# Expert index lists written to memory as three rows of 384 bytes, transposed on the PE first

## The chip, the cores and the metric

The kernel runs on one core of a Trainium2 chip. The metric is the time of one execution in microseconds (us), as the median of several runs. A separate execution was taken with the hardware profiler; its rows are in a section below. The engines are the PE (matrix products), the DVE (vector), the ACT (scalar functions), the POOL (GpSimd) and the SP, which issues most transfers. Each engine works through its own instructions in order. Transfers issued by the SP run on the hardware queue q1, indirect ones issued by the POOL on the software queue q0; both are served by the same 16 DMA engines.

## The reference, cut to what matters

Three stages follow each other: attention with pooled queries; a mixture of 8 experts with a capacity of 288 tokens each; a dense block with a softmax-weighted activation and layer norm.

```python
def _moe_ref(x, w_gate, w1, w2):          # x: 2304 x 512, 8 experts, F = 1024
    cap = N // E                          # 288
    logits = x @ w_gate
    order = np.argsort(-logits.flatten())
    for idx in order:                     # greedy: best pairs first
        tok, e = (int(idx) // E, int(idx) % E)
        if assigned[tok] >= 0 or counts[e] >= cap:
            continue
        assigned[tok] = e
        counts[e] += 1
    for e in range(E):
        mask = assigned == e
        out[mask] = np.maximum(x[mask] @ w1[e], 0.0) @ w2[e]

def _moe2_ref(x, w_in, w_out, g_ln):
    h = x @ w_in
    solu = h * softmax(h)
    return (layernorm(solu) * g_ln) @ w_out
```

Each expert takes exactly 288 tokens, so the experts' outputs, one after the other, are 18 blocks of 128 rows, and the dense block works on them in that order. Its results go back to the rows of the tokens.

## The kernel before, in words

Attention and the gate's logits come first and take the first half of the time. The tokens' vectors lie in memory as `xd`. The second half (class `Moe`) goes through the experts, in an order that the routing itself decides.

**Routing** (`Router.phase`, one phase for each expert). Which expert fills up next, and with which tokens, is found on the DVE by comparing keys with thresholds and on the PE by counting, in rounds: `cmp`, a matmul, `ge`, a matmul, `jm`. The end of a phase makes the expert's list of tokens: each token's slot, then a matmul over 18 chunks (L695) into PSUM, from which the DVE copies `idf6` (L698) and computes the 288 indices as a tile `ix` of 96 partitions by 3 (L699). The generator `phase` yields between engines; each piece is an entry of the schedule below, named `f`, `t`, `s`, `a`, `i` (the index matmul) and `x` (the DVE's part). `upd` then brings the routing state up to date.

**The list** is used twice. The POOL gathers the tokens' rows with three indirect transfers of 96 rows of 2 KB (`g_row`, into `h`). And the SP writes the list to memory as a part of `tab` (`g_tab`, L770), from where `e2_ix` later loads it in another division, 128 indices to a block, as `ixb`; with these the POOL scatters the finished rows to the output (`e2_st`, L880).

**The expert.** The PE transposes the gathered rows (`g_tr`, L776), the ACT splits each tile into a high part (`xh`) and the DVE makes the low part (`xl`). Weights come as `raw` blocks of 512 KB, eight to an expert (`w_load`), in three buffers; the ACT makes the high part `wh` (`w_hi`, L766), the DVE the low part `wl` (L769). First product: `c_mm` (L790), with `hh` and `hl` behind it; second: `d_mm` (L804), with `yh` (L808) and `yl` (L810).

**The dense block** takes each finished block of 128 rows: `e1_mm` (L816), then `e1_h`, maximum, exponent, `zz`, mean and variance on ACT and DVE, transposes (L856), `e2_mm` (L870), `e2_o` and the scatter.

**The order** on every engine is fixed before the kernel runs. `Moe.run` describes each operation with an engine, an assumed duration, a priority, what it needs and which buffers it takes and frees; the list scheduler `Sched` plays that through and emits the operations in the order of its result. Entry `gt` is the write of the list, `gr` the gathers, `wd` a weight load, `gx` the transposes, `cm` and `dm` the two products, `m1` and `m2` those of the dense block. The engines then run that order with real waits.

Of the kernel before, what the change touches and what calls it, by code (L numbers as in the profile page):

```python
# [14 lines left out]
ALU = mybir.AluOpType  # L15
# [4 lines left out]
I32=DT.int32  # L20
# [5 lines left out]
class Sched:  # L26


    def __init__(s,bufs,lat=195,cold=0,begin=600.0):
        s.bufs=dict(bufs); s.lat=lat if isinstance(lat,dict) else dict.fromkeys(('X','PE','ACT','DVE','POOL','SP'),lat); s.cold=cold; s.begin=begin; s.ops=[]; s.name={}; s.free0={}  # L30
        s.same=dict(X=0,PE=0,ACT=155,DVE=128,POOL=105,SP=200)
    def op(s,key,eng,dur,pri,f,need=(),alloc=(),free=(),late=0,slack=0,lock=0,until=0.0):
        assert key not in s.name,key
        o=dict(key=key,eng=eng,dur=dur,pri=pri,f=f,need=list(need),alloc=list(alloc),free=list(free),late=late,slack=slack,until=until,lock=lock or eng=='POOL',i=len(s.ops),ready=0.0,succ=[],t=None)
        s.ops.append(o); s.name[key]=o
# [500 lines left out]
I32=DT.int32  # L536
NT=18; E=8; CAP=288
NEG=-3.0e38
ROUNDS=((2048<<16,31),(64<<16,31),(1<<16,63),(2048,31),(64,31),(1,64))
def route_consts(tc,C):  # L540
    nc=tc.nc; c={}
    def it(name,shape,pattern,base,cm,dt=F32):
        t=C.tile(shape,dt,name=name)
        nc.gpsimd.iota(t,pattern=pattern,base=base,channel_multiplier=cm,allow_small_or_imprecise_dtypes=True)
        return t
    c['w8']=it('w8',[128,8],[[-1,8]],8,0)
    ms=C.tile([64,6],BF,name='ms')
    for n,(st,J) in enumerate(ROUNDS):
        u=st>>16 or st
        c['thr',n]=it(f'thr{n}',[128,J],[[u,J]],u if n<5 else 0,0)  # L550
        if n<3: nc.vector.tensor_scalar(c['thr',n],c['thr',n],65536.0,None,op0=ALU.mult)
        nc.vector.memset(ms[:,n:n+1],-float(st))
    c['ms']=ms
    c['i96']=it('i96',[128,96],[[1,96]],0,0)
    c['i3']=it('i3',[128,3],[[1,3]],0,0)
    c['chv']=it('chv',[128,NT],[[1,NT]],0,0)
    c['pv']=it('pv',[128,1],[[0,1]],0,1)
    jp=it('jp',[128,128],[[1,128]],0,-1)
    c['tri']=C.tile([128,128],BF,name='tri'); nc.vector.tensor_scalar(c['tri'],jp,0.0,None,op0=ALU.is_gt)
    c['ones']=C.tile([128,128],BF,name='onesb'); nc.vector.memset(c['ones'],1.0)  # L560
    return c
class Router:
    def __init__(s,tc,C,W,ps,L,consts):
        s.tc=tc; s.nc=nc=tc.nc; s.W=W; s.ps=ps; s.L=L; s.c=consts
        s.neg=C.tile([128,E],F32,name='neg'); nc.vector.memset(s.neg,0.0)
        s.rem=C.tile([128,E],F32,name='rem'); nc.vector.memset(s.rem,float(CAP))
        s.un=C.tile([128,NT],F32,name='un'); nc.vector.memset(s.un,1.0)
        s.asg=C.tile([128,NT,E],F32,name='asg'); nc.vector.memset(s.asg,0.0)
        s.idx={}; s.ev={}; s.rest=None
        s.A=C.tile([128,NT,128],BF,name='A'); nc.gpsimd.memset(s.A,0.0)  # L570
    def t(s,name,shape,dt=F32,bufs=2): return s.W.tile(shape,dt,name=name,bufs=bufs)
    def psum(s): return s.ps.tile([128,512],F32,name='rt',bufs=1)
# [5 lines left out]
    def phase(s,k):  # L578

        nc=s.nc; V=nc.vector; c=s.c; last=(k==E-1)  # L580
        f=s.t('f',[128,E]); fm=s.t('fm',[128,1]); f2=s.t('f2',[128,E])
        sl=s.t('sl',[128,2,NT],BF); tmp=s.t('tmp',[128,NT,E],bufs=1)
        if not last:
# [18 lines left out]
            for n,(st,J) in enumerate(ROUNDS):  # L602
# [14 lines left out]
                p=s.psum()  # L617
# [6 lines left out]
                p=s.psum()  # L624
# [15 lines left out]
        gt=s.t('gt',[128,2,NT])  # L640
# [7 lines left out]
            V.tensor_tensor(tmp,oh,s.be(f2),op=ALU.mult)  # L648
            ohf=s.t('ohf',[128,NT]); s.red(ohf,tmp,ALU.add)
        if k>0:  # L650
            tm2=s.t('tm2',[128,NT,E],bufs=1)
            V.tensor_tensor(tm2,s.asg,s.be(f2),op=ALU.mult)
            asf=s.t('asf',[128,NT]); s.red(asf,tm2,ALU.add)
        if k==0:
# [10 lines left out]
        p=s.psum()  # L665
# [27 lines left out]
        p=s.psum()  # L693
# [3 lines left out]
        idf=s.t('idf6',[96,6]); ix=s.t('ix',[96,3],I32,bufs=8)  # L697
        V.tensor_copy(idf,p[:96,:6])  # L698
        V.scalar_tensor_tensor(ix,idf[:,0:3],128.0,idf[:,3:6],op0=ALU.mult,op1=ALU.add)  # L699
        s.idx[k]=ix  # L700
        s.rest=None
        if not last: s.rest=(inr,key,gt,oh,f2)
    def update(s):
# [25 lines left out]
class Moe:  # L729
# [37 lines left out]
    def w_lo(s,k,i,e,j):  # L767
        nc=s.nc; hi,lo=s.wt[k,i]; raw=s.raw[k,i]; c=slice(j*512,j*512+512)
        (nc.vector if e=='V' else nc.gpsimd).tensor_tensor(lo[:,c],raw[:,c],hi[:,c].bitcast(F32),op=ALU.subtract)  # L769
    def g_tab(s,k): s.nc.sync.dma_start(s.tab[k*CAP:(k+1)*CAP].rearrange("(c a) -> a c",a=96),s.rt.idx[k])  # L770
    def g_row(s,k,c):
        x=s.xg[k,c]=s.W.tile([128,512],F32,name='h2',bufs=HB)[:96]
        s.nc.gpsimd.indirect_dma_start(out=x,out_offset=None,in_=s.x,in_offset=bass.IndirectOffsetOnAxis(ap=s.rt.idx[k][:,c:c+1],axis=0))
# [107 lines left out]
    def run(s):  # L881
# [4 lines left out]
        def op(key,eng,dur,pri,f,*a,**kw): X.op(key,eng,dur,pri+M['off'].get(key[0],0),lambda: f(*a),**kw)  # L886
# [6 lines left out]
        def seg(key,eng,dur,pri,g,need=()):  # L893
            nonlocal last
            op(key,eng,dur,pri,lambda: next(g(),None),lock=eng=='DVE' and dur<2000 and dur>600,need=list(need)+([last] if last else []))
            last=key
        J=[31,31,63,31,31,64]
        for k in range(E):
# [3 lines left out]
            p=-2e6 if k==0 else S0+PER*(k-1)+M['rp']  # L902
            ps=0 if k==0 else M['rs']
            i=0
            def sg(name,eng,dur,g):
                nonlocal i
                seg(('r',k,name),eng,dur,p+ps*i,g); i+=1
            if k>0:
                def u0(k=k): start(k); return s.up
                sg('u0','DVE',1165,u0); sg('u1','PE',25,lambda: s.up); sg('u2','DVE',281,lambda: s.up)  # L910
                ph=lambda k=k: s.ph[k]
            else:
                def ph0(): start(0); return s.ph[0]
                ph=lambda: s.ph[0]
            if k<E-1:
                for n in range(6):
                    g0=ph0 if k==0 and n==0 else ph
                    sg(('d',n),'DVE',{0:3200}.get(n,100+139+(710 if J[n]<63 else 1340)),g0)
                    sg(('p',n),'PE',480,ph); sg(('g',n),'DVE',77,ph); sg(('q',n),'PE',7,ph)
            sg('f','DVE',2541 if k<E-1 else 900,ph); sg('t','PE',60,ph); sg('s','DVE',2900,ph); sg('a','DVE',1940,ph); sg('i','PE',428,ph); sg('x','DVE',250,ph)  # L920
            ix=('r',k,'x')
            b0=S0+PER*k
            op(('wr',k),'SP',300,b0+M['wd'],s.w_reg,k,need=[('r',k,'f')])
            for i_ in range(8):
# [3 lines left out]
                e=M['lo' if k else 'lo0'][i_]  # L928
                for j in range(2):
                    op(('wl'+e,k,i_,j),'DVE' if e=='V' else 'POOL',605 if e=='V' else 1250,tn+M['wl']+j,s.w_lo,k,i_,e,j,lock=1,need=[('wh',k,i_)]+([('r',0,'x') if e=='V' else ('gr',0,2)] if k==0 else []),free=[(('wd',k,i_),'raw')])  # L930
            op(('gt',k),'SP',480,-1e6,s.g_tab,k,need=[ix],late=1800)
            for c in range(3): op(('gr',k,c),'POOL',1038,-1e6+c,s.g_row,k,c,need=[ix]+([('cm',k-1,1,1)] if k else []),alloc=['h2'],late=7300)
            for dc in range(4):
                op(('gx',k,dc),'PE',246,b0+M['gx'],s.g_tr,k,dc,need=[('gr',k,c) for c in range(3)]+([('gx',k,0)] if dc else []),alloc=['tr'] if dc else ['tr','x'],free=[(('gr',k,c),'h2') for c in range(3)])
# [3 lines left out]
            for f in range(8):  # L938
                t=b0+1500*f
# [5 lines left out]
            c=(k*CAP)%128; nb=(k*CAP+CAP)//128-(k*CAP)//128; bb=(k*CAP)//128  # L945
# [4 lines left out]
            for d in range(4):  # L950
                for h in range(4):
                    t=b0+12000+750*(4*d+h)
# [3 lines left out]
                t=b0+12000+1500*(2*d+1)  # L956
                op(('dh',k,d),'ACT',291,t,s.d_hi,k,d,c,need=[('dm',k,d,3)]+([('cy',k)] if c else [])+ye)
                op(('dl',k,d),'DVE',369,t,s.d_lo,k,d,c,need=[('dh',k,d)],free=[(('dm',k,d,0),'cd')])
            for j in range(nb):
# [6 lines left out]
                t=t1+5200+M['ec']  # L966
# [30 lines left out]
def whole(tc, q, k, v, w_gate, w1, w2, w_in, w_out, g_ln, out):  # L997
    nc = tc.nc
    if w_in.dtype == DT.int64:
        w_in, w_out = [a.bitcast(I32).rearrange("a (b t) -> a b t", t=2) for a in (w_in, w_out)]  # L1000
    with tc.tile_pool(name="dr", bufs=1, space=bass.MemoryType.DRAM) as DR, tc.tile_pool(name="c", bufs=1) as C, \
            tc.tile_pool(name="rt", bufs=2) as RT:
        xd = DR.tile([2304, 512], F32, name="xd")
        tab = DR.tile([2304], I32, name="tab")
        wst = DR.tile([2, 512, 1024], F32, name="wst")
        wso = DR.tile([2, 1024, 512], F32, name="wso")
        idf = C.tile([128, 128], F32, name="idf")
        make_identity(nc, idf)
        L = C.tile([128, 18, 8], F32, name="L")
        consts = route_consts(tc, C)  # L1010
        with tc.tile_pool(name="ps", bufs=1, space=PS) as ps, tc.tile_pool(name="ca", bufs=1) as CA:
            wg = CA.tile([128, 4, 8], F32, name="wg")
            nc.sync.dma_start(wg, w_gate.rearrange("(c p) e -> p c e", p=128))
            gs = CA.tile([128, 16], F32, name="gs")
            nc.sync.dma_start(gs[:, 0:8], g_ln.rearrange("(c p) -> p c", p=128))
            nc.gpsimd.tensor_scalar(gs[:, 8:16], gs[:, 0:8], 2.0**-52, 1.0, op0=ALU.mult, op1=ALU.mult)
            attention(tc, idf, q, k, v, xd, wg, L, ps, w_in, wst, w_out, wso, gs)
        with tc.tile_pool(name="w", bufs=2) as W, tc.tile_pool(name="ps2", bufs=1, space=PS) as ps, \
                tc.tile_pool(name="r", bufs=1) as R:
            rt = Router(tc, C, RT, ps, L, consts)  # L1020
            Moe(tc, R, W, ps, xd, w1, w2, wst, wso, out, tab, rt, idf).run()


# [26 lines left out]
```

## Time and profile before

| | us |
|---|---|
| median of 3 runs | 1085.98 |
| lowest and highest run | 1085.26, 1086.63 |
| the profiled execution, its own time | 1089.18 |
| its span, first to last instruction | 1087.4 |
| PE busy | 981.4 (90%) |
| DVE busy | 795.6 (73%) |
| ACT busy | 683.5 (63%) |
| POOL busy | 544.3 (50%) |

The busy times are sums over the whole span. The profiled execution takes 3.2 us more than the median of the runs, so differences are worked out within it and then set against the median. Attention ends near 540 us; from there on the order of work is that of the second scheduler.

### The profile page before, as it was taken

What the parts mean: (1) busy time and instruction counts of PE and PEld (TensorE: products, weight loads), DVE (VectorE), ACT (ScalarE), POOL (GpSimd) and SP (SyncE); (2) the same over time, 40 slices, a digit from 0 to 9 for tenths busy, and PEclk for the clock granted to TensorE, in tenths of its full rate; (3) what the DMA queues carried; (4) which work ended last, traced back from release to release, by engine and by line L of the source; (5) the groups of instructions that cost most, each with busy time, mean ns of one, the idle gap of its engine ahead of it and who ended that gap; (6) DMA issues with size and microseconds to landing.
All of it is one profiled execution on the core that took longest, in us unless ns stands there. A gap on an engine that the chain in (4) does not pass through costs nothing. (4 is left out here: it accounts for less than half of the span.)

```text
span 1087.4 us, 26325 instructions
## 1 busy us (share of the span) xinstructions
PE 981.4 (90%) x10274; PEld 876.9 (81%) x10274; DVE 795.6 (73%) x1954; ACT 683.5 (63%) x1314; POOL 544.3 (50%) x574
## 2 busy tenths in 40 slices
PE   4899999999899999999429897989989899899997
PEld 3689989899799988898418796978968788789985
DVE  5799998998779798986587786767757657555332
ACT  3689988999889988999313353426253452465343
POOL 6789999999979989977541111011100111111011
PEclk9899999999989999999759998999999999899999
DMA  5845445544534333222577515243241413552000
GB/s 148 262 109 155 109 118 151 150 125 106 160 103 122 104 102 104 74 69 70 186 180 253 98 55 112 72 100 98 51 136 51 105 54 60 108 158 69 11 21 30
DMA packets 118317, 118.14 MB, mean 109 GB/s; under 512 B 15216, under 2 KB 93168, under 8 KB 118192
## 3 DMA queue, kind: packets, MB, share of 16 engines
q1 hardware_dynamic: 115216, 107.02, 36.7%
q0 software_dynamic: 2976, 9.44, 3.3%
q8 instruction: 81, 1.33, 0.5%
q14 instruction: 44, 0.36, 0.1%
HBM read 84.44 MB, written 17.84 MB: 94 GB/s over the span
## 5 line engine op out<-in xcount | busy, mean ns | idle before, releaser
L304 POOL TENSOR_TENSOR pl<-pf,ph 128x576 f16<-128x576 f32 x192 | 254.5, 1345 | 35.9 <-ACT pf L299 26.9
L262 DVE TENSOR_REDUCE mx<-aux 128x1 f32<-128x384 f32 x420 | 215.4, 547 | 32.3 <-PE aux L257 23.8
L294 ACT ACTIVATE ph<-big 128x576 f16<-128x576 f32 x288 | 187.4, 660 | 47.7 <-PE big L290 45.1
L289 PE MATMUL big<-QM,K 128*128 128x288 f32 x576 | 178.8, 326 | 12.3 <-DVE pl L305 8.1
L290 PE MATMUL big<-QLH,KHL 128*128 128x288 f32 x576 | 163.3, 299 | 0.0
L313 PE MATMUL acc<-VH,ph 128*128 128x65 f16 x1440 | 128.4, 196 | 0.6 <-DVE xb L325 0.5
L766 ACT ACTIVATE wh<-raw 128x1024 fp32r<-128x1024 f32 x64 | 67.4, 1054 | 97.3 <-DMA raw<-in_moe_w_dram 75.9
L289 PEld LDWEIGHTS big<-QM,K 128*128 128x128 f32 x576 | 110.9, 193 | 21.6 <-DVE pl L305 12.3
L257 PE MATMUL aux<-KHL,QM 128*128 128x384 f32 x372 | 122.0, 376 | 4.6 <-DVE mx L262 3.1
L299 ACT ACTIVATE pf<-big 128x576 f32<-128x576 f32 x192 | 125.6, 666 | 0.9 <-POOL pl L304 0.7
L314 PE MATMUL acc<-VL,ph 128*128 128x64 f16 x1440 | 126.0, 194 | 0.0
L313 PEld LDWEIGHTS <-ph 128*128 128x128 f16 x1440 | 95.5, 98 | 20.7 <-issue 5.4
L290 PEld LDWEIGHTS big<-QLH,KHL 128*128 128x128 f32 x576 | 111.3, 193 | 0.0
L314 PEld LDWEIGHTS <-ph 128*128 128x128 f16 x1440 | 98.5, 98 | 0.1
L317 PE MATMUL acc<-VH,pl 128*128 128x65 f16 x1440 | 91.3, 194 | 0.9 <-DVE pl L305 0.6
L305 DVE TENSOR_TENSOR pl<-big,ph 128x576 f16<-128x576 f32 x96 | 71.8, 749 | 23.2 <-ACT big L300 18.3
L790 PE MATMUL cd<-xh,wh 128*128 128x288 f32 x256 | 82.3, 321 | 1.8 <-DVE hl L796 1.7
L769 DVE TENSOR_TENSOR wl<-raw,wh 128x512 fp32r<-128x512 f32 x120 | 79.4, 684 | 6.0 <-ACT wh L766 6.0
L850 POOL TENSOR_SCALAR sm<-sm 128x1 f32<-128x1 f32 x18 | 5.1, 281 | 151.7 <-ACT h L847 151.7
L804 PE MATMUL cd<-hh,wh 128*128 128x288 f32 x256 | 77.4, 302 | 0.0
L790 PE MATMUL cd<-xl,wh 128*128 128x288 f32 x256 | 77.2, 301 | 0.0
L790 PE MATMUL cd<-xh,wl 128*128 128x288 f32 x256 | 76.8, 300 | 0.0
(237 smaller groups left out, 2685.2 us busy)
## 6 DMA issues: line engine op xcount, KB each, us to landing
raw<-in_moe_w_dram SPq DMA_DIRECT2D x64, 512.0 KB
kt<-in_k_dram SPq DMA_DIRECT2D x32, 288.0 KB
vt<-in_v_dram SPq DMA_DIRECT2D x32, 288.0 KB
K<-KHL SPq DMA_DIRECT2D x32, 288.0 KB
qa<-in_q_dram SPq DMA_DIRECT2D x32, 256.0 KB
QM<-QLH SPq DMA_DIRECT2D x31, 144.0 KB
raw<-in_moe_w_in_dram SPq DMA_DIRECT2D x16, 256.0 KB
xd<-xb SPq DMA_DIRECT2D x4, 1024.0 KB
```

The costliest lines, as they stand in the source:

```text
L257: nc.tensor.matmul(p[:,j,:384],QM[i][:,o:o+128],KHL[i][:,ks],start=True,stop=True)
L262: nc.vector.reduce_max(o,st[h]['pm',u][:,:len(un),:384],axis=AX.X)
L289: nc.tensor.matmul(p[:,j,:288],K1[i][:,c*128:(c+1)*128],QM[i][:,QO+j*288:QO+(j+1)*288],start=True,stop=False)
L290: nc.tensor.matmul(p[:,j,:288],KHL[i][:,c*128:(c+1)*128],QLH[i][:,j*288:(j+1)*288],start=False,stop=True)
L294: nc.scalar.activation(two(x['h']),x['p'][:,:,:288],AF.Exp,scale=0.0625)
L299: nc.scalar.activation(two(x['f']),x['p'][:,:,:288],AF.Exp,scale=0.0625)
L304: if KIND[g%len(KIND)]=='P': nc.gpsimd.tensor_tensor(x['l'],x['f'],x['h'],op=ALU.subtract)
L313: nc.tensor.matmul(acc[:,b,:],ph[:,s],VH[i][:,c],start=(c==0 and b==0),stop=False,skip_group_check=True)
L314: nc.tensor.matmul(acc[:,b,:64],ph[:,s],VL[i][:,c],start=False,stop=False,skip_group_check=True)
L317: nc.tensor.matmul(acc[:,b,:],pl[:,s],VH[i][:,c],start=False,stop=(c==NCK-1),skip_group_check=True)
L769: (nc.vector if e=='V' else nc.gpsimd).tensor_tensor(lo[:,c],raw[:,c],hi[:,c].bitcast(F32),op=ALU.subtract)
L790: nc.tensor.matmul(p[:,:CAP],a[:,dc,cs],b[:,dc],start=(dc==0 and n==0),stop=(dc==3 and n==2))
```

## The change

The list no longer goes to memory from `ix`, where each index is an element of its own at a distance of 384 bytes from its neighbour's target. The DVE computes it a second time as floats (`vf`), the PE transposes that with the identity matrix into 3 rows of 96, the DVE copies them as integers into `row`, and the SP writes three rows of 96 indices. The gathers use `ix` as before. In the schedule, the new pieces `y` (PE) and `w` (DVE) stand behind `x`, and the write waits for `w`. To make room, `tm2` is put into the buffer of `tmp`.

```diff
-    def __init__(s,tc,C,W,ps,L,consts):
-        s.tc=tc; s.nc=nc=tc.nc; s.W=W; s.ps=ps; s.L=L; s.c=consts
+    def __init__(s,tc,C,W,ps,L,consts,idn):
+        s.idn=idn; s.tc=tc; s.nc=nc=tc.nc; s.W=W; s.ps=ps; s.L=L; s.c=consts
...
-        s.idx={}; s.ev={}; s.rest=None
+        s.idx={}; s.row={}; s.ev={}; s.rest=None
...
-            tm2=s.t('tm2',[128,NT,E],bufs=1)
+            tm2=s.t('tmp',[128,NT,E],bufs=1)
...
         V.scalar_tensor_tensor(ix,idf[:,0:3],128.0,idf[:,3:6],op0=ALU.mult,op1=ALU.add)
+        vf=s.t('vf',[96,3]); V.scalar_tensor_tensor(vf,idf[:,0:3],128.0,idf[:,3:6],op0=ALU.mult,op1=ALU.add)
         s.idx[k]=ix
+        yield
+        p=s.psum()
+        nc.tensor.transpose(p[:3,:96],vf,s.idn[:96,:96])
+        yield
+        s.row[k]=s.t('row',[3,96],I32,bufs=1); V.tensor_copy(s.row[k],p[:3,:96])
...
-    def g_tab(s,k): s.nc.sync.dma_start(s.tab[k*CAP:(k+1)*CAP].rearrange("(c a) -> a c",a=96),s.rt.idx[k])
+    def g_tab(s,k): s.nc.sync.dma_start(s.tab[k*CAP:(k+1)*CAP].rearrange("(c a) -> c a",a=96),s.rt.row[k])
...
-            sg('f','DVE',2541 if k<E-1 else 900,ph); sg('t','PE',60,ph); sg('s','DVE',2900,ph); sg('a','DVE',1940,ph); sg('i','PE',428,ph); sg('x','DVE',250,ph)
+            sg('f','DVE',2541 if k<E-1 else 900,ph); sg('t','PE',60,ph); sg('s','DVE',2900,ph); sg('a','DVE',1940,ph); sg('i','PE',428,ph); sg('x','DVE',340,ph); sg('y','PE',60,ph); sg('w','DVE',90,ph)
...
-            op(('gt',k),'SP',480,-1e6,s.g_tab,k,need=[ix],late=1800)
+            op(('gt',k),'SP',480,-1e6,s.g_tab,k,need=[('r',k,'w')],late=1800)
```

In the changed kernel the lines behind L706 have numbers that are 6 higher (L804 is L810, L769 is L775).

The DVE's order at the end of expert 1's phase, before:

```order
L769 TENSOR_TENSOR wl<-raw,wh 128x512 x2
L698 COPY idf_12577<-rt 96x6
L699 SCALAR_TENSOR_TENSOR ix<-idf_12577 96x3
L712 TENSOR_TENSOR og<-oh,gt 128x144
L577 TENSOR_REDUCE cn<-og 128x8
```

and in the changed kernel:

```order
L775 TENSOR_TENSOR wl<-raw,wh 128x512 x2
L698 COPY idf_12583<-rt 96x6
L699 SCALAR_TENSOR_TENSOR ix<-idf_12583 96x3
L700 SCALAR_TENSOR_TENSOR vf<-idf_12583 96x3
L775 TENSOR_TENSOR wl<-raw,wh 128x512
L816 TENSOR_TENSOR yl<-cd,yh 128x288
L706 CAST row<-rt 3x96
L775 TENSOR_TENSOR wl<-raw,wh 128x512
L718 TENSOR_TENSOR og<-oh,gt 128x144
```

Between `vf` and `row`, while the PE transposes, stand a half weight block and a `yl`; the state's update (`og`, `cn`) begins behind `row`.

The PE's order behind the index matmuls of expert 3 (`cd<-hh,wh` and the like are products of `d_mm`), before:

```order
L695 LDWEIGHTS A
L695 MATMUL rt<-Bv,A 128x6
L804 MATMUL cd<-hh,wh 128x288
L804 MATMUL cd<-hl,wh 128x288
L804 MATMUL cd<-hh,wl 128x288
L804 MATMUL cd<-hh,wh 128x288
L804 MATMUL cd<-hl,wh 128x288
L804 MATMUL cd<-hh,wl 128x288
L804 MATMUL cd<-hh,wh 128x288
```

and in the changed kernel:

```order
L695 LDWEIGHTS A
L695 MATMUL rt<-Bv,A 128x6
L810 MATMUL cd<-hh,wh 128x288
L810 MATMUL cd<-hl,wh 128x288
L810 MATMUL cd<-hh,wl 128x288
L810 MATMUL cd<-hh,wh 128x288
L810 MATMUL cd<-hl,wh 128x288
L810 MATMUL cd<-hh,wl 128x288
L704 MATMUL rt<-idf,vf 3x96
L810 MATMUL cd<-hh,wh 128x288
```

The transpose of the list stands six products behind the index matmuls; at experts 1 and 2 it is twelve, at the others more.

The SP's order around the list of expert 2 (`ISA` rows set registers for the load behind them), before:

```order
L762 DMA raw<-in_moe_w_dram 128x4x256
L762 ISA
L762 DMA raw<-in_moe_w_dram 128x4x256
L770 DMA tab<-ix 96x3x1
L873 DMA ixb<-tab 128x1
L762 ISA
L762 DMA raw<-in_moe_w_dram 128x4x256
```

and in the changed kernel:

```order
L768 DMA raw<-in_moe_w_dram 128x4x256
L768 ISA
L768 DMA raw<-in_moe_w_dram 128x4x256
L768 ISA
L768 DMA raw<-in_moe_w_dram 128x4x256
L776 DMA tab<-row 3x96
L879 DMA ixb<-tab 128x1
L768 ISA
L768 DMA raw<-in_moe_w_dram 128x4x256
```

The third weight block has moved ahead of the list. It is so for experts 2, 4 and 6; for 1, 3, 5 and 7 two weight blocks stand ahead of the list, as before. Elsewhere the same operations stand in nearly the same order, with pieces exchanged at each expert; at expert 1 the first transposes of gathered rows stand behind nine operations of `e1_mm` instead of twelve.

## Rows read from the trace of the kernel before

**Rows 1.** The page, part 1: busy time, share of the span, instructions of each engine.

```profile
PE 981.4 (90%) x10274; PEld 876.9 (81%) x10274; DVE 795.6 (73%) x1954; ACT 683.5 (63%) x1314; POOL 544.3 (50%) x574
```

**Rows 2.** A stretch: PE, PEld, DVE, ACT, POOL busy; clock, DMA share, GB/s.

```profile
660.00:690.00 30.00, 24.38 (x151) 19.75 (x150) 16.97 (x48) 13.36 (x24) 5.26 (x7) 0.89 0.57 126
```

**Rows 3.** What the PE waited for from 594 us on: total, times, longest.

```profile
PE e L816 <- ACT yh L808: 9.7, 3, 4.8
PE rt L625 <- DVE ge L622: 5.6, 1, 5.6
PE tr L776 <- DMA h<-xd,ix: 3.8, 5, 1.5
PE rt L619 <- DVE cmp L612: 3.4, 2, 1.8
PE tr L776 <- DVE xl L781: 2.0, 2, 1.4
...
PE cd L790 <- DVE hl L796: 1.7, 2, 1.4
```

**Rows 4.** The same of the ACT, from 594 us on.

```profile
ACT wh L766 <- DMA raw<-in_moe_w_dram: 66.8, 14, 9.0
```

**Rows 5.** Timeline of the SP's queue at expert 6: start, duration, what.

```profile
905.30 1.05 SPq L762 DMA_DIRECT2D raw<-in_moe_w_dram  x2
915.71 0.34 SPq L770 DMA_DIRECT2D tab<-ix  x1
916.32 0.99 SPq L762 DMA_DIRECT2D raw<-in_moe_w_dram  x2
```

**Rows 6.** Timeline of the ACT there; in brackets the idle time ahead and its end.

```profile
909.02 1.06 ACT L766 ACTIVATE wh<-raw 128x1024 fp32r<-128x1024 f32 x1 [1.96 <-DMA raw<-in_moe_w_dram]
...
927.43 1.06 ACT L766 ACTIVATE wh<-raw 128x1024 fp32r<-128x1024 f32 x1 [8.21 <-DMA raw<-in_moe_w_dram]
928.39 0.39 ACT L808 ACTIVATE yh<-cd 128x288 fp32r<-128x288 f32 x1
```

**Rows 7.** Timeline of the PE there.

```profile
928.84 0.80 PE L816 MATMUL e<-winh,yh 128*128 128x512 f32 x1 [4.81 <-ACT yh L808]
```

**Rows 8.** Timelines of ACT and DVE at expert 2.

```profile
671.58 1.06 ACT L766 ACTIVATE wh<-raw 128x1024 fp32r<-128x1024 f32 x1 [8.07 <-DMA raw<-in_moe_w_dram]
673.16 0.69 DVE L824 TENSOR_REDUCE sm<-e 128x1 f32<-128x512 f32 x1 [5.85 <-ACT h L820]
```

**Rows 9.** DMA queues from 602.2 to 611 us, behind expert 1's list.

```profile
DMA packets 580, 0.28 MB, mean 32 GB/s; under 512 B 304, under 2 KB 580, under 8 KB 580
...
q1 hardware_dynamic: 580, 0.28, 57.9%
```

**Rows 10.** DMA queues from 906 to 910 us, two weight blocks with no list.

```profile
DMA packets 1057, 1.06 MB, mean 264 GB/s; under 512 B 32, under 2 KB 1056, under 8 KB 1056
...
q1 hardware_dynamic: 1056, 1.05, 76.6%
```

**Rows 11.** DMA queues from 611 to 617 us, behind the stretch of rows 9.

```profile
q0 software_dynamic: 192, 0.59, 36.0%
```

**Rows 12.** The gathers, line 773, all 24.

```profile
DMA to landing us min/median/max: 9.5/12.0/13.5
```

**Rows 13.** The scatters of results, line 880, all 18.

```profile
DMA to landing us min/median/max: 2.7/3.0/9.6
```

**Rows 14.** Stretches at the lower clock behind PE stalls, first and last of five.

```profile
620.60:627.10 6.50, 5.94 (x23) 4.87 (x22) 4.77 (x13) 3.27 (x8) 0.00 (x0) 0.50 0.54 158
...
928.80:934.20 5.40, 5.37 (x13) 4.21 (x14) 5.01 (x21) 2.63 (x4) 0.00 (x0) 0.50 0.66 150
```

**Rows 15.** Timeline of the PE: three transposes of gathered rows.

```profile
680.80 0.41 PE L776 MATMUL tr<-idf,h 96*128 96x96 f32 x3
```

**Rows 16.** Timelines of PE and DVE at the end of expert 3's phase.

```profile
717.20 0.61 PE L695 MATMUL rt<-Bv,A 128*128 128x6 bf16 x18
718.49 0.15 DVE L698 COPY idf<-rt 96x6 f32<-96x6 f32 x1
```

More of the change, by code (lines that the diff above doesn't have):

```diff
@@ L1019, in whole @@
                 tc.tile_pool(name="r", bufs=1) as R:
-            rt = Router(tc, C, RT, ps, L, consts)
+            rt = Router(tc, C, RT, ps, L, consts, idf)
             Moe(tc, R, W, ps, xd, w1, w2, wst, wso, out, tab, rt, idf).run()
```

## The prediction

> **What bounds the kernel now.** I read the page first: the PE is busy 90% of the span [rows 1], so only the other tenth, and stretches at the lower clock, can be won without taking matmuls out. Attention, to about 540 us, is untouched by the change. From 594 us on the experts follow each other, and I went through that time in stages of 30 us: at each change of expert one falls short, like that from 660 us, with the PE busy for 24.4 us and a clock of 0.89 [rows 2].
>
> The waits of the PE name the loss [rows 3]: products of e1 wait 9.7 us for yh from the ACT, one router matmul 5.6 us for ge from the DVE, the gather's transposes 3.8 us for the gathered rows, router matmuls 3.4 us for cmp. In the same stretch the ACT waits 66.8 us in 14 waits for raw weights, 9.0 us the longest [rows 4]. Expert 6 shows how the two hang together. The SP issues the list at 915.71 and two weight blocks from 916.32 [rows 5]. The ACT, which runs in order, stands at the split of the first block for 8.21 us until 927.43, and only behind it copies yh at 928.39 [rows 6]; the PE, out of work since 924.03, goes on at 928.84 after 4.81 us [rows 7]. Eleven us pass from issue to split. The pair issued at 905.30, with no list ahead of it, is split at 909.02: 3.7 us [rows 5, 6].
>
> At expert 2 the same wait reaches the PE through the DVE: the split waits 8.07 us, and the DVE, waiting 5.85 us for the ACT's h behind it, is late with ge [rows 8].
>
> So what holds the weights? In the 8.8 us after expert 1's list, 580 packets moved at 32 GB/s: 304 under 512 bytes (the list's 288 elements and few others), 0.28 MB in all, and none of the software queue, although all three gathers had been issued [rows 9]. In the 4 us after 906, without a list, 1057 packets moved 1.06 MB at 264 GB/s [rows 10]. Once the list is through, the gather's 0.59 MB goes by, beside the weights, within 6 us [rows 11]. The gather takes 12.0 us from issue to landing (least 9.5), while the scatter of results, the same kind of indirect transfer on the same queue, takes 3.0 [rows 12, 13]. So some 9 us after each list nearly nothing else gets through.
>
> **What the list costs, and how sure that is.** 580 packets at 57.9% of 16 engines over 8.8 us are 81.5 engine-us. A weight packet costs 76.6% x 16 x 4 us / 1056 = 46 ns [rows 10]; the 276 others of the 580 would be 12.8 engine-us, so a list element stands for (81.5 - 12.8)/304 = 226 ns, against 46 ns for a packet with 250 times the bytes. By length, 8.8 us for 288 elements are 31 ns each, one after the other.
>
> [...]
>
> **The change part by part.**
>
> *The write itself.* 288 elements become 3 rows. Before shows no such store. Bounds: a packet of weights (46 ns) and a whole list's hold (8.8 us). I take the low end, since the rows have three destinations and not 288, and the nearest packet in size is the weights' [rows 10].
>
> [...]
>
> *Weights and gathers then.* Without the hold, two blocks and a gather are 1.05 + 0.59 MB [rows 10, 11]; at 264 GB/s that is 6.2 us, alone 3.7 us. At expert 6: 916.32 + 6.2 + 1.4 (from split to PE, 927.43 to 928.84) = 923.9, just before the PE runs dry at 924.03. The gather needs some 3.5 us of issues and then 3.0 to 6.2 us to land, under 10 us, and the PE has 11 to 14 us of matmuls between the index matmuls and the first transposes. So the four waits above go: 9.7 + 5.6 + 3.8 + 3.4 = 22.5 us [rows 3]. What stays is what has nothing to do with the list: xl, 2.0 in 2 waits, and hl, 1.7 in 2.
>
> *The clock.* [...] First and last of the five: 5.94 us busy at 0.50, and 5.37 at 0.50 [rows 14]. Half of the busy time at half clock is lost: 3.0 and 2.7 us; all five come to 3.0 + 1.75 + 1.6 + 1.7 + 2.7 = 10.7 us. No stall, no fall: 10.7 us come back.
>
> *Added on the PE.* Eight transposes; three of the gather's, of 96x96, take 0.41 us [rows 15], so 8 x 0.14 = 1.1 us, all on the path since the PE is full.
>
> *The hand-offs.* PE to DVE (vf) to PE (transpose) to DVE (row). The PE is in order: if vf is late, the d products behind the transpose wait. At expert 3 the index matmul ends at 717.81, and the DVE starts idf at 718.49 [rows 16]; ix and vf follow at steps of some 0.2 us, so vf would end near 719.0, and six products (six times 0.13 us) bring the PE to 718.6: 0.4 us and the passing on. The other experts have 1.3 us and more of work in between. Bounds: nothing, and 1.7 us each (the longest wait for hl is 1.4, all of them 1.7). I take 1.2 us for all eight.
>
> *On the DVE.* vf, row: 16 instructions near 0.2 us, 3 us in 490, hidden where the DVE is busy 17 of 30 us [rows 2]; without that cover, 3 us. tm2 now uses tmp's buffer, on one engine in order: nothing.
>
> *On the SP.* The list now waits for row, some 1 to 2 us after ix, and what is queued behind it waits too: the third and fourth weight block, the ixb loads, with the ACT behind the weights. In experts 2, 4 and 6 the third block has moved ahead of the list; in 1, 3, 5 and 7 it stands behind. Against 5 us won, 1 to 2 us are inside the slack, except where the ACT stands first in line.
>
> *The start.* At expert 0 the PE waits for the next phase's route on the DVE anyway; I take nothing, bounds 1 us lost to 1.5 us won.
>
> *What is late next.* The stalls that the list does not explain measure about 1 us (2.0/2, 1.7/2). The order of the scheduler's table shifts a little at each expert. I allow one such stall at each of six boundaries: 6 us.
>
> **Sum.** 22.5 + 10.7 - 1.1 - 1.2 - 6 = 24.9 us. The profiled execution took 1089.18 us (span 1087.4), so it would take 1064.3. It is 3.2 us above the median of the runs, 1085.98; there the sum gives 1061.1. I say **1061 us**.
>
> **The rivals.**
>
> *The gather is what blocks, not the list* (slower). List and gather always come together, so the trace cannot part them. For it: the gather's 12 us. Against it: in the slow 8.8 us no packet of the software queue moved [rows 9], and once it ran it went at a normal pace. Then weights land no earlier, the list holds the SP for 1 to 2 us more at four experts (4 x 1.5 = 6), and transposes and hand-offs cost 2.3: 1086 + 8 = 1094 us. It decides if the slow stretch stays longer than 7 us. Chance 8%. [...]
>
> *Three rows hold the queues as long* (it doesn't do what it says): 1086 + 2.3 = 1088 us. [...] Against it: three pieces for 288. Chance 5%.
>
> *The list was it, but the time is given back*: the ACT and DVE are late next, the row holds the SP, or stalls shrink but are still followed by the low clock. Then only the gather's 3.8 us, part of the rest and little of the clock come back: 3 to 14 us, say 1077 us. For it: the ACT waits 66.8 us, and the PE feels only a third of that, so chains are long. Chance 16%.
>
> *No change at all*, losses and gains cancelling: 1086 us, 3%.
>
> *The forecast*: 68%, with its own range 1052 to 1072: at the low end no allowance and no hand-offs (33.2 + 1.5 - 1.1 = 33.6), at the high end 14 us won.
>
> **How the numbers follow.** A measurement of this kernel can tell some 0.2% (2.2 us) from no change. Faster: 68 + 16 + 2 of the small ones = 86%; same 4%; slower 10%. The range reaches from 1050 (the whole 33.6 and a little of the start) to 1080, which leaves out the slower cases and a little of the third.
>
> **What would show it.** Right: in the 9 us after each list more than 150 GB/s; gathers landing under 8 us; the ACT's waits for raw under 25 us; PE waits for yh and the gathered rows under 3 us; no or one stretch at half clock between 594 and 1050 us. Hand-offs: waits of the transpose for vf, of the list for row. Wrong: a slow stretch of 7 us or more after the list (first two rivals), or a short one with the same sum of PE waits under other names (third).

## The result, and the profile after

The changed kernel takes 1053.5 us (median of 4 runs, 1052.33 to 1055.31) against 1085.86 (4 runs, 1085.26 to 1086.63): ratio 0.9703, 95% interval 0.9686 to 0.9721. The forecast was 1061; the gain is 32.4 us instead of 24.9. The profiled execution took 1052.33 us, its span is 1050.5.

The page, part 1, of the changed kernel answers [rows 1]:

```profile
PE 965.8 (92%) x10282; PEld 866.4 (82%) x10282; DVE 798.6 (76%) x1970; ACT 683.1 (65%) x1314; POOL 545.7 (52%) x574
```

Eight transposes more on the PE, and yet 15.6 us less of busy time; 11.7 of them lie behind 594 us, where the stretches at half clock [rows 14] are gone. Stretches from 594 us to the last PE instruction, columns as in [rows 2], before:

```profile
594.00:1081.06 487.06, 459.14 (x3230) 401.35 (x3229) 306.10 (x890) 218.87 (x406) 63.55 (x87) 0.97 0.32 79
```

and after, with a stage of 30 us that holds expert 2's list:

```profile
594.00:1044.19 450.19, 447.45 (x3237) 394.19 (x3236) 308.28 (x904) 219.38 (x406) 66.93 (x87) 1.00 0.28 85
...
647.00:677.00 30.00, 30.00 (x220) 26.06 (x220) 26.41 (x76) 18.93 (x35) 5.57 (x7) 1.00 0.39 115
```

The PE's idle time falls from 487.06 - 459.14 = 27.92 us to 2.74, its busy time by 11.69: 36.9 us between the two profiled executions. Between the medians it is 32.4, since the profiled execution of before ran 3.2 us above its median and that of the changed kernel 1.2 us below. The clock's mean goes from 0.97 to 1.00; the stretches of [rows 14] have no counterpart. What the PE still waits for from 594 us on, answering [rows 3]:

```profile
PE rt L666 <- DVE sl L661: 1.9, 2, 1.7
PE e L876 <- ACT zh L866: 0.9, 2, 0.5
PE rt L619 <- DVE oh L610: 0.6, 1, 0.6
PE rt L704 <- DVE vf L700: 0.3, 1, 0.3
```

None of the four waits of the forecast is left, nor xl and hl. The ACT's wait for weights from 594 us on [rows 4], the landing of the gathers [rows 12], and the DMA queues in the 8.8 us behind expert 1's list [rows 9], after:

```profile
ACT wh L772 <- DMA raw<-in_moe_w_dram: 8.8, 6, 3.5
```

```profile
DMA to landing us min/median/max: 3.9/4.6/6.7
```

```profile
DMA packets 1880, 1.89 MB, mean 214 GB/s; under 512 B 230, under 2 KB 1736, under 8 KB 1880
...
q1 hardware_dynamic: 1688, 1.30, 55.6%
q0 software_dynamic: 192, 0.59, 27.8%
```

Where 0.28 MB had moved, now 1.89 MB do, the whole gather among them.

One thing went the other way. At the start, where expert 1's route is searched beside the first weights, timelines of DVE and POOL of the changed kernel show:

```profile
556.66 8.45 DVE L607 TENSOR_TENSOR cmp<-key,thr 128x558 bf16<-128x558 f32 x1
```

```profile
557.15 7.36 POOL L775 TENSOR_TENSOR wl<-raw,wh 128x512 fp32r<-128x512 f32 x6
```

That comparison takes 0.74 us elsewhere. Before, the next operation but one stood so, for less, beside a shorter run:

```profile
559.60 5.65 DVE L610 TENSOR_TENSOR oh<-Lm,un 128x144 bf16<-128x144 f32 x1
```

```profile
560.16 4.92 POOL L769 TENSOR_TENSOR wl<-raw,wh 128x512 fp32r<-128x512 f32 x4
```

From expert 0's first index matmul to the first expert product it is 21.6 us, 19.5 before: 2.1 us lost.

### The profile page after: what moved, and what is told of

Its sections match the earlier page's. It is cut to its first block, busy times and chain, and to the rows that moved or that the text cites. A ratio compares the mean times of both kernels' runs of the same rounds, so it can differ in the third digit from the quotient of the medians.

```text
span 1050.5 us, 26365 instructions
## 1 busy us (share of the span) xinstructions
PE 965.8 (92%) x10282; PEld 866.4 (82%) x10282; DVE 798.6 (76%) x1970; ACT 683.1 (65%) x1314; POOL 545.7 (52%) x574
## 5 line engine op out<-in xcount | busy, mean ns | idle before, releaser
L304 POOL TENSOR_TENSOR pl<-pf,ph 128x576 f16<-128x576 f32 x192 | 253.6, 1339 | 37.1 <-ACT pf L299 27.8
L775 DVE TENSOR_TENSOR wl<-raw,wh 128x512 fp32r<-128x512 f32 x120 | 79.5, 685 | 5.8 <-ACT wh L772 5.8
L810 PE MATMUL cd<-hh,wh 128*128 128x288 f32 x256 | 77.7, 304 | 0.0
L257 PEld LDWEIGHTS aux<-KHL,QM 128*128 128x128 f32 x372 | 67.4, 193 | 11.4 <-DVE mx L262 4.5
```

The costliest lines, as they stand in the source:

```text
L257: nc.tensor.matmul(p[:,j,:384],QM[i][:,o:o+128],KHL[i][:,ks],start=True,stop=True)
L304: if KIND[g%len(KIND)]=='P': nc.gpsimd.tensor_tensor(x['l'],x['f'],x['h'],op=ALU.subtract)
```

## The experiments

Theory, as the prediction has it: the 288 single elements hold both queues, each in its turn, so the time goes with their number. Rivals: each such store has a fixed hold; what counts is where the elements lie; the new order or the wait for `row` brings the gain, not the form of the store. All runs in one table. "Start" is from expert 0's first index matmul to the first expert product, "rest" from there to the last PE instruction, both from the profile; attention ahead of them varies by several us between executions (that matmul comes at 548.1 us in e7 and at 557.6 in e5), so the rest parts the kernels best; it is that of one execution each, and that of before ran 3.2 us above its median. "Gathers" is the median from issue to landing, "raw" the ACT's wait for weights from 594 us on.

| run | time, us (range) | ratio to before, interval | start | rest | gathers | raw |
|---|---|---|---|---|---|---|
| before | 1085.86 | | 19.5 | 508.1 | 12.0 | 66.8 |
| changed | 1053.5 | 0.9703, 0.9686 to 0.9721 | 21.6 | 471.9 | 4.6 | 8.8 |
| e1 | 1068.39 (1064.0 to 1070.0) | 0.9856, 0.9804 to 0.9908 | 20.2 | 487.9 | 11.2 | 36.4 |
| e2 | 1049.34 (1047.4 to 1053.29) | 0.9701, 0.9648 to 0.9753 | 20.9 | 470.2 | 3.2 | 6.1 |
| e3 | 1073.31 (1069.7 to 1077.19) | 0.9932, 0.9897 to 0.9966 | 20.4 | 491.3 | 9.8 | 40.5 |
| e4 | 1054.68 (1052.68 to 1055.27) | 0.9738, 0.9690 to 0.9786 | 21.6 | 471.6 | 5.4 | 6.1 |
| e5 | 1053.37 (1051.12 to 1056.2) | 0.9728, 0.9681 to 0.9776 | 20.9 | 469.5 | 5.1 | 15.7 |
| e6 | 1055.86 (1053.53 to 1057.54) | 0.9751, 0.9706 to 0.9796 | 21.6 | 472.6 | 5.0 | 6.8 |
| e7 | 1064.83 (1060.62 to 1068.71) | 0.9853, 0.9799 to 0.9908 | 19.9 | 484.4 | 9.1 | 37.1 |
| e8 | 1055.24 (1052.43 to 1057.44) | 0.9744, 0.9699 to 0.9789 | 14.9 | 478.8 | - | - |
| e9 | 1053.31 (1051.99 to 1058.26) | 0.9751, 0.9724 to 0.9777 | 16.6 | 477.7 | - | - |
| e10 | 1052.3 (1050.41 to 1058.48) | 0.9748, 0.9719 to 0.9777 | 16.3 | 476.2 | - | - |
| e11 | 1054.41 (1051.74 to 1058.05) | 0.9740, 0.9692 to 0.9787 | 21.6 | 472.4 | 5.2 | 7.0 |
| e12 | 1053.74 (1051.14 to 1056.8) | 0.9742, 0.9693 to 0.9791 | 21.6 | 471.8 | 5.5 | 8.1 |

Each ratio is against runs of the kernel before on the same chip, whose medians lay between 1080.5 and 1085.9.

### e1: the old store in the new order

```diff
-    def g_tab(s,k): s.nc.sync.dma_start(s.tab[k*CAP:(k+1)*CAP].rearrange("(c a) -> c a",a=96),s.rt.row[k])
+    def g_tab(s,k): s.nc.sync.dma_start(s.tab[k*CAP:(k+1)*CAP].rearrange("(c a) -> a c",a=96),s.rt.idx[k])
```

> The changed kernel, its order, transposes and waits kept, but the list leaves as 288 single elements again (from ix). Theory L (the store of single elements holds both queues, some 9 us for each list): the slow stretch is back, under 60 GB/s for 8 to 9 us behind each list, and the time is 1078 to 1092 us. Rival O (the shifted order and the later list brought the gain, not the form of the store): 1052 to 1058 us, no slow stretch.

The time lies between the two ranges: about half of the loss comes back with the old store, not all. The slow stretch does come back: gathers 11.2 us, some 9 us under 100 GB/s behind seven of the eight lists. What differs is how much of it is felt: the ACT waits 36.4 us for weights, not 66.8. The new order seems to cover part of the hold; that it is the third block ahead of the list at three experts that does it fits, but was not tried apart.

### e2: three rows in the old order

The kernel before; the rows come from a constant tile filled at the start, so its list needs no index and leaves some 8 us earlier. It leaves out the list itself: finished rows go to the wrong tokens. As in the changed kernel, `tm2` lies in the buffer of `tmp`.

```diff
+        lf=C.tile([24,96],F32,name='lf'); nc.gpsimd.iota(lf,pattern=[[1,96]],base=0,channel_multiplier=96,allow_small_or_imprecise_dtypes=True)
+        s.lst=lf.bitcast(I32); nc.vector.tensor_copy(s.lst,lf)
...
+    def g_tab(s,k): s.nc.sync.dma_start(s.tab[k*CAP:(k+1)*CAP].rearrange("(c a) -> c a",a=96),s.rt.lst[3*k:3*k+3])
```

> The kernel before, its order kept and no transposes, but three rows of 96 indices leave from a constant tile at the list's place. What it changes: the list in memory is the identity, so finished rows go to other tokens. Theory L: no slow stretch, gathers land in under 7 us, 1048 to 1056 us; the distance to the changed kernel (1053.5) is the price of transposes and hand-offs, 1 to 4 us. Rival O: 1080 to 1088 us.

The whole gain is there without the new order, the detour over the PE and the wait for `row`: the ratios of e2 and of the change agree. Since its list also leaves earlier, e5 repeats it without that.

### e3: a third of the elements

```diff
+        t=s.tab[k*CAP:(k+1)*CAP].rearrange("(c a) -> c a",a=96)
+        s.nc.sync.dma_start(t[0:1].rearrange("c a -> a c"),s.rt.idx[k][:,0:1])
+        s.nc.sync.dma_start(t[1:3],s.rt.row[k][1:3])
```

> The changed kernel, but the first third of the list leaves as 96 single elements and two thirds as two rows. Theory L by count (31 ns an element, 8.8 us / 288): a slow stretch of 3 us behind each list, which the slack of some 5 us hides for the most part, 1054 to 1062 us. If a store of elements holds the queues for a fixed time whatever its count: 8 to 9 us, 1075 to 1090 us.

The theory by number falls: 96 elements cost as much as 288 (1073.3 against 1068.4 us in e1). Six us of e3, from 2 us behind its list for expert 3 on (at 709.38):

```profile
DMA packets 239, 0.26 MB, mean 43 GB/s; under 512 B 0, under 2 KB 234, under 8 KB 239
...
q1 hardware_dynamic: 234, 0.24, 73.6%
q0 software_dynamic: 5, 0.02, 6.3%
```

No packet under 512 bytes is in this stretch: the elements' packets are over, and still little moves.

### e4, e6, e11, e12: all 288 elements, farther apart

The changed kernel; the elements leave from `ix`, and the table has room between them: 512 bytes from element to element in e4, 64 in e6, 32 in e11, 16 in e12 (4 in e1). The diff is that of e4; in e6, e11 and e12 the table is 16, 8 and 4 wide instead of 128.

```diff
-        tab = DR.tile([2304], I32, name="tab")
+        tab = DR.tile([2304, 128], I32, name="tab")
...
+    def g_tab(s,k): s.nc.sync.dma_start(s.tab[k*CAP:(k+1)*CAP,0:1].rearrange("(c a) o -> a c o",a=96),s.rt.idx[k][:,:,None])
```

The distance that counts is not the 384 bytes named with the change above. That is the distance between the three indices of one partition; those of neighbouring partitions go to neighbouring places, 4 bytes apart, in the kernel before as in e1. These four runs widen both.

> As e1, 288 single elements in the new order, but 512 bytes apart in memory instead of side by side. Theory L by count: within 4 us of e1 and the same slow stretch. Rival C (elements side by side, written by 16 engines at once, hinder each other at the same place in memory): the slow stretch is under 3 us and the time 1053 to 1062 us.

> The changed kernel with the list sent as 288 single elements from the index tile, 64 bytes apart in memory instead of 512. If the elements hold each other up only when they share a piece of memory of 64 bytes or less: 1052 to 1057 us, as with 512 bytes. If the piece that they share is larger (a 512-byte piece then holds 8 of them instead of 96 or 128): between, 1056 to 1066 us, with a slow stretch of some 1 to 5 us after each list.

> The changed kernel with the list sent as 288 single elements from the index tile, 32 bytes apart. 64 and 512 bytes apart cost nothing (1055.9 and 1054.7 us). If the piece of memory that elements must not share is 32 bytes or less: 1052 to 1057 us and no slow stretch. If it is 64 bytes: two elements in each, 1057 to 1066 us, and a slow stretch of 2 to 6 us after each list.

> The same with 16 bytes apart. If the hold grows with the number of elements in a piece of 64 bytes (four here, 16 where they lie side by side, which gave 1068.4 us in this order of code): 1057 to 1066 us, a slow stretch of 3 to 7 us. If any sharing costs the whole hold: 1066 to 1072 us and 8 to 9 us. If the piece is 16 bytes or less: 1052 to 1057 us.

All four take as long as the changed kernel (1053.7 to 1055.9 us against 1053.5), with as many single elements as before, so a fixed hold for each such store falls too. The DMA queues of the kernel before at expert 3's list, for 2 us from its issue at 718.86 and for the 7 us behind them:

```profile
DMA packets 351, 0.05 MB, mean 25 GB/s; under 512 B 304, under 2 KB 351, under 8 KB 351
```

```profile
DMA packets 196, 0.20 MB, mean 29 GB/s; under 512 B 0, under 2 KB 196, under 8 KB 196
```

and the same two stretches in e4, from 708.72 on:

```profile
DMA packets 343, 0.04 MB, mean 21 GB/s; under 512 B 304, under 2 KB 343, under 8 KB 343
```

```profile
DMA packets 1353, 1.60 MB, mean 228 GB/s; under 512 B 224, under 2 KB 1209, under 8 KB 1353
...
q1 hardware_dynamic: 1161, 1.01, 44.7%
q0 software_dynamic: 192, 0.59, 30.1%
```

In both kernels the same 304 small packets are through within 2 us. Then 196 packets pass in the one and 1353 in the other. So no element's packet is slow in the profile; what stands is the weights and gathers behind elements that lie 4 bytes apart.

The packets are quick, within 2 us, and the rival that the gathers block, and not the list, is false: the same gathers land in 5.4 us in e4, against 12.0 before.

At 16 bytes a little of the hold is left, too little for the time to show. The second and third microsecond from the list of expert 3 on in e12, and the third in e4:

```profile
709.08:710.08 1.00, 1.00 (x9) 1.00 (x9) 0.96 (x7) 0.61 (x1) 0.91 (x1) 1.00 0.05 0
710.08:711.08 1.00, 1.00 (x10) 1.00 (x9) 0.97 (x4) 0.12 (x1) 0.79 (x1) 1.00 0.64 15
```

```profile
710.72:711.72 1.00, 1.00 (x10) 1.00 (x9) 0.96 (x4) 0.11 (x1) 0.79 (x1) 1.00 0.75 236
```

Counted so at expert 3, from the issue of the list on, 9 microseconds stay under 100 GB/s in the kernel before, in e1 and in e3, 6 in e7 (8 bytes), 3 in e12, and 2 in e11, e6, e4 and the changed kernel. In these counts the hold shrinks with the distance and does not end at a step.

### e7: three rows, elements 8 bytes apart

```diff
+        tab = DR.tile([2304, 2], I32, name="tab")
...
+    def g_tab(s,k): s.nc.sync.dma_start(s.tab[k*CAP:(k+1)*CAP,0:1].rearrange("(c a) o -> c a o",a=96),s.rt.row[k][:,:,None])
```

> The changed kernel with its three transposed rows, but the table has 8 bytes for each number, so that each row leaves as 96 single 4-byte elements 8 bytes apart, all from three partitions. If elements close together hold the queues whichever partition they come from: 1062 to 1076 us, as with single elements from 96 partitions (1068.4 and 1073.3). If it takes many engines writing to the same place, and elements from three partitions go through few engines, the hold falls on few engines: 1053 to 1060 us, with less than 3 us under 150 GB/s after each list.

The hold is back, though the elements come from three partitions: for some 6 us behind most lists mostly under 100 GB/s. Six us from 2 us behind expert 3's list, e7 and, from its own list at 707.08, the changed kernel:

```profile
DMA packets 657, 0.63 MB, mean 106 GB/s; under 512 B 165, under 2 KB 615, under 8 KB 657
...
q0 software_dynamic: 58, 0.17, 44.5%
q1 hardware_dynamic: 599, 0.46, 38.6%
```

```profile
DMA packets 1360, 1.61 MB, mean 268 GB/s; under 512 B 224, under 2 KB 1216, under 8 KB 1360
...
q1 hardware_dynamic: 1168, 1.02, 54.8%
q0 software_dynamic: 192, 0.59, 31.8%
```

Three source rows are no cure (1064.8 us); rows written in one piece are (1053.5). Elements 8 bytes apart hold for less long than at 4 bytes and longer than at 16, but the source differs too between e7 and the others, so what the distance alone does at 8 bytes is not shown.

### e5: the old order with the elements 512 bytes apart

The kernel before with e4's table and store, nothing else: no transpose, no `vf`, no `row`.

> The kernel before in its own order and with the list sent straight from the index tile (no transpose, no hand-off, the list still waits for the indices), and one edit: the table in memory has 512 bytes for each of its numbers, so the 288 elements lie 512 bytes apart. Theory (the hold comes from elements that lie side by side; the form of the store alone brings the gain, the detour and the new order bring nothing of their own): 1047 to 1054 us, no stretch under 150 GB/s after a list beyond 3 us, PE waits for yh and gathered rows under 3 us in all. Rival (in the old order the list needs the identity's earlier start, as the run with constant rows had it, or the new order, to be harmless): 1060 to 1075 us.

It equals the changed kernel (0.9728 against 0.9703, intervals overlapping). So the new order, the detour and the eight transposes neither bring nor cost anything that the times show once the hold is gone (the rest is some 2 us shorter without them, in one execution each). That the order mattered in e1 only because there was a hold to cover fits.

### e8, e9, e10: the start

The low weight parts of expert 0 move from the POOL to the DVE: all (e8, shown), or two blocks more (`V V P V V V P V`), in the changed kernel (e9) and in e5 (e10).

```diff
-    lo0=['P', 'P', 'P', 'V', 'V', 'V', 'P', 'V'],
+    lo0=['V', 'V', 'V', 'V', 'V', 'V', 'V', 'V'],
```

> The changed kernel with the low weight parts of expert 0 all on the DVE (three of its eight blocks now; the other five are on the POOL). Theory (the comparison at L607 took 8.45 us instead of 0.74 us because the POOL ran six subtractions in a row beside it): L607 of expert 1 takes 0.7 to 1 us, and from the index matmul of expert 0 to its first expert matmul it is 13 to 17 us instead of 20.6, so 1046 to 1051 us. Rival (the DVE's ten more subtractions of 0.6 us, and what they push back, eat what the POOL gives free): 1052 to 1057 us.

> The changed kernel with the low parts of two more blocks of expert 0 (the first and second) on the DVE; two blocks stay on the POOL. With all eight on the DVE the first expert matmul came 14.9 us after the index matmul (21.5 in the changed kernel), and the rest took 478.8 us instead of 471.9, mostly lost in the first 60 us to a DVE that was late. Theory (the POOL's work beside L607 costs the start, too much on the DVE costs what follows; a division between keeps part of both): 15 to 18 us to the first matmul, 472 to 475 us after it, 1048 to 1052 us. Rival (what the start gains is given back whatever the division, since the search of expert 1 and the weights set the pace there): 1052 to 1056 us.

> The kernel before, its list sent straight from the index tile with elements 512 bytes apart, and the same two blocks of expert 0 moved from the POOL to the DVE. In the old order L607 of expert 1 was not hit (0.74 us) but L610 stood behind the POOL's run, and the first matmul came 20.9 us after the index matmul, the rest took 469.6 us. Theory: 15 to 18 us and 470 to 473 us, 1046 to 1051 us, the fastest of all. Rival (given back, as above): 1051 to 1056 us.

The expectation of e8 miscounts: in the changed kernel four blocks of expert 0 are on the POOL and four on the DVE. The cause of the long comparison is confirmed. DVE timeline of e8, with no subtraction on the POOL:

```profile
563.63 0.74 DVE L607 TENSOR_TENSOR cmp<-key,thr 128x558 bf16<-128x558 f32 x1
```

The start is shorter by 6.7 us, and the rest longer by 6.9: the gain is given back, and the rival holds in e9 and e10 too. PE waits of e8 from 566 to 640 us (the same wait is 0.5 us in the changed kernel), and the 30 us from its first expert product on, then the same 30 us of the changed kernel:

```profile
PE rt L625 <- DVE ge L622: 4.4, 2, 3.8
```

```profile
570.50:600.50 30.00, 26.03 (x217) 24.26 (x216) 17.01 (x47) 7.25 (x15) 0.00 (x0) 0.86 0.54 179
```

```profile
572.30:602.30 30.00, 28.17 (x247) 26.69 (x246) 22.68 (x67) 10.21 (x17) 2.58 (x2) 0.92 0.47 158
```

The products start earlier and then wait for the DVE; the PE has 2.1 us less work in these 30 us, at a lower clock. But the DVE is not overloaded: it stands at a low part for which the weights have not come. Timelines of ACT, DVE and PE of e8, and its stretch from 572 to 582 us:

```profile
585.71 1.06 ACT L772 ACTIVATE wh<-raw 128x1024 fp32r<-128x1024 f32 x1 [5.03 <-DMA raw<-in_moe_w_dram]
```

```profile
586.80 1.29 DVE L775 TENSOR_TENSOR wl<-raw,wh 128x512 fp32r<-128x512 f32 x2 [4.84 <-ACT wh L772]
```

```profile
588.21 0.16 PE L625 MATMUL rt<-ge,ms 31*128 31x8 bf16 x1 [3.76 <-DVE ge L622]
```

```profile
572.00:582.00 10.00, 10.00 (x76) 9.34 (x74) 6.43 (x15) 2.59 (x5) 0.00 (x0) 0.81 1.05 387
```

All 16 DMA engines are busy there, at 387 GB/s, with the dense block's weights (`woh`, `wol`) in the same queue, and expert 0's next block comes late. The same chain stands in e9 and e10: the ACT waits 4.5 and 5.8 us for weights, the DVE 5.0 and 5.6 us behind it, the PE 3.7 and 4.8 us. So here the weights set the pace, as the rival of e9 has it. No version of the twelve is measurably faster than the changed kernel.

## Why the prediction was right or wrong

**What held.** The place (the list, not the gathers), the chain from late weights over the ACT to the PE, the four waits and the five stretches at half clock as one loss, and the signs asked for: 214 GB/s in the 8.8 us behind expert 1's list, gathers under 8 us, 8.8 us of waits for weights, no wait for yh and gathered rows, no half clock between 594 and 1050 us. Only the mean of more than 150 GB/s is missed behind the lists of experts 2 and 4 (some 126 GB/s over 9 us), where the queues were empty after about 6 us. The first two rivals fall by these; the third (given back later) by the sum.

**The step that failed: how an element holds the queues.** "31 ns each, one after the other" and "226 ns" of engine time laid the whole slow stretch on the elements' own packets. They are through in 2 us of the 9; with 96 elements the hold is as long (9 us in e3), and with 288 it is gone at 32 bytes and more (2 us in e4, e5, e6 and e11, as in the changed kernel) and nearly so at 16 (3 us in e12). The step went wrong by charging a stretch to the packets that were counted in it, without looking when in the stretch they ran. The choice of the low bound for three rows rested on "three destinations and not 288": the value was right, the reason not; 288 destinations cost as little, if they lie apart.

**The sizes.** From 594 us on, 25.2 us of idle time and 11.7 of busy time went, 36.9 in all between the profiled executions; the forecast had 22.5 - 6 - 1.2 = 15.3 and 10.7 - 1.1 = 9.6, 24.9 in all. The range held with a term that was 6 us too cautious.
- *What is late next*: 6 us allowed, and nothing came. The waits for xl and hl, put down to other causes, went as well: 25.2 - 22.5 = 2.7 us of idle time beyond the four waits.
- *Hand-offs*: 1.2 us; the waits for vf from 594 us on are 0.3 us in one. Allowance, further waits and hand-offs make up the idle time that was missed: 6 + 2.7 + 1.2 = 9.9 us.
- *Added on the PE*: 1.1 us, near enough. The records of the transposes last 0.246 us (median of eight), but they overlap those of the products, as at expert 1 (PE timeline, start and duration):

```profile
602.41 0.29 PE L810 MATMUL cd<-hh,wl 128*128 128x288 f32 x1
602.54 0.25 PE L704 MATMUL rt<-idf,vf 96*3 96x96 f32 x1
602.57 0.38 PE L810 MATMUL cd<-hh,wh 128*128 128x288 f32 x1
602.78 0.29 PE L810 MATMUL cd<-hl,wh 128*128 128x288 f32 x1
```

Products start 0.13 to 0.14 us apart. With a transpose between them, two steps take 602.78 - 602.41 = 0.37 us instead of 0.27, so an estimated 0.1 us each and 0.8 for eight.

- *The clock*: 10.7 us were forecast; busy time fell by 11.7 with the transposes in it. What makes the difference is open.
- *The start*: nothing taken, 1 us lost as bound; 2.1 us lost, outside the bound. As e8 to e10 show, what is won there is given back, so the 2.1 us need not be lost in the sum either.
- *On the SP*: the wait of the list for `row` costs nothing that e5, which does without it, would show.

**Open.** What goes on in those 7 us is not in the trace. The hold goes with the distance between the elements (9 us at 4 bytes in e1, 3 at 16 in e12, 2 at 32 in e11) and not with their number (9 us for 96 in e3 as for 288 in e1). What in the distance brings it about, no run shows.

## What to carry to other kernels

When a transfer seems to block others, count its packets in slices of a microsecond: whether they run through the whole slow stretch, or are long gone in it, are two causes with two cures. Single 4-byte stores side by side in memory are to be avoided even where they are few and off the path: 96 of them for each list took 1073.3 us (e3). Rows in one piece (1053.5 us) and a spacing of 16 to 512 bytes (1053.4 to 1055.9 us in e4, e5, e6, e11 and e12) did equally well in time, and the spacing needs no engine. An allowance for "what is late next" belongs where what stands behind has no reserve. From 594 us on there was reserve: DVE and ACT were busy for 308 and 219 of 450 us, and the DMA engines for 28%. At the start, where the DMA engines were full (387 GB/s over 10 us in e8), each of three attempts gave its gain back.

## What the runs showed of the hardware

- At expert 3, the packets of 288 stores of 4 bytes, 4 bytes apart, were over within 2 us, and yet weights and gathers kept to some 30 GB/s for about 7 us more; 96 did the same (43 GB/s in e3). From the issue on, the time under 100 GB/s was 9 us at 4 bytes, 6 at 8 bytes (from three partitions), 3 at 16, and 2 at 32, 64 and 512 bytes, as with three rows.
- A DVE operation of two operands, 0.74 us elsewhere, took 8.45 us beside six POOL subtractions in a row (7.36 us), and 0.74 again without them (e8). Its record spans the whole run of six, and not one of them, of 7.36 / 6 = 1.23 us; it ends 0.60 us behind the run, at 556.66 + 8.45 = 565.11 against 557.15 + 7.36 = 564.51.
